# A gated linear-attention kernel: the subtraction of a column maximum moved from two vector engines into an accumulating DMA, and one more batch's attention in float32

## The chip, the cores and the metric

The kernel runs on one core of a Trainium2 chip. The metric is the device time of one execution in microseconds (us). A core has five engines with an instruction queue each: TensorE (PE, matrix products; PEld is its weight load), VectorE (DVE), ScalarE (ACT), GpSimd (POOL) and SyncE (SP), which here only issues DMA transfers. Each engine takes its instructions in the order in which they stand in its queue; an instruction that waits holds up all behind it. 16 DMA engines move data between the chip's memory (HBM) and the on-chip memory.

## The reference

Eight batches, eight heads, 576 tokens, head size 64 (512 channels in all), everything float32:

```python
q_s = exp(q - max(q, axis=-1));  q_s /= sum(q_s, axis=-1) + 1e-9     # softmax over the 64 channels of a head
k_s = exp(k - max(k, axis=2));   k_s /= sum(k_s, axis=2) + 1e-9      # softmax over the 576 tokens
kv  = einsum('bhsd,bhse->bhde', k_s, v)
x   = einsum('bhsd,bhde->bhse', q_s, kv)                             # heads put side by side: 512 channels
gate = sigmoid(causal 5-tap convolution of x over tokens, one filter per channel)
out  = (gate * (x @ w_val)) @ w_out
```

The maximum of k that matters here is taken for each of the 512 channels over 576 tokens; it is one row of 512 numbers for a batch.

## The kernel before, in words

A batch's tokens lie on the 128 partitions as four blocks of 128, and a tail of 64 (two batches share one tail tile). The program is a list of steps, `ORDER`, written out in full in the source: each step is a small function that issues the instructions of one tile, with a letter for the engine where there is a choice (`v` DVE, `a` ACT, `p` POOL). Every engine gets its instructions in the order of that list, and so does the DMA queue of SP.

One batch b goes through these steps. `load_q`, `load_v`, `load_k` (1 MB each, all from SP); `q_max`, `q_sub`, `q_exp`, `q_sum`, `q_mul` make the softmax of q. For k: `load_km b j` loads four tiles with channels on partitions, `k_peak` reduces each to its maxima (DVE), `k_row` writes the 512 maxima as one row to HBM, `k_spread` reads that row back onto all 128 partitions, `k_sub` (POOL or DVE, five per batch) subtracts it from the k tile, `k_exp` (ACT) takes the exponential. `kv` is the product of k and v on PE, `kv_norm` its division by the sums; `q_turn` and `q_turned` transpose q; `attend` (four per batch) makes x in PSUM. From each x tile come `x_high` and `x_low` (a rounded part and the rest, so that float32r products keep the accuracy), `first` and four `tap`s (the convolution; `tap v` is one DVE instruction, `tap a` is a product on ACT and a sum on POOL), and `sigmoid`. `value` (four per batch, 24 matmuls each, line 542) needs all `x_high` and `x_low` of its batch; `gated` multiplies by the gate, `g_high` and `g_low` split again, `project` (four per batch, 24 matmuls each, also line 542) needs all of these, and `store` copies and writes out.

Batches 0 and 1 take k another way (`load_kc`, `k_top`, `k_raise`, `k_turn`), with channels on partitions and a transposition on PE. `F32_BATCHES` names the batches whose `attend` is one float32 product instead of three float32r ones; for the others `kv_high`, `kv_low` and `q_low` prepare the parts. In the first 50 us the weights are also unpacked (`load_words`, `part`, `field`, `scaled`, `signed`, `joined`, `w_high`, `w_low`).

k, q and v tiles have two buffers each, the shared k tail one, the km tiles three (shared with the unpacking of weights).

## Time and profile before

| what | us |
|---|---|
| median of 3 runs (321.49 to 322.12) | 322.0 |
| the profiled execution | 320.3 |
| its span, first to last instruction | 318.5 |
| PE busy | 297.3 (93%) |
| DVE busy | 271.5 (85%) |
| ACT busy | 204.6 (64%) |
| POOL busy | 188.7 (59%) |
| first `value` product starts at | 45.55 |

The lines of the profile give an engine, an operation, the tile written and the tiles read, the shape, and how often. Behind the bar stand the busy time and the mean of one instruction in ns, then the idle time of the engine just before and what ended it.

### The profile page before, as it was taken

The numbers are of one execution on the slowest core, as the hardware profiler recorded it, in microseconds if no ns is written. First come the engines' busy times: TensorE is split into PE (matmuls) and PEld (weight loads), VectorE is DVE, ScalarE is ACT, GpSimd is POOL, SyncE is SP. The second block draws the span as 40 slices with busy tenths as digits, with TensorE's granted clock in tenths as the row PEclk, the third lists the DMA queues.
The fourth block names the chain that finished last, engine by engine and source line by source line (L and its number), as shares of the span: only waits on it lengthen the run. The fifth ranks groups of instructions, "written<-read, shape, count | busy, mean of one in ns | idle before, by whom it ended". The sixth has DMA issues, their size and how long they took to land.

```text
span 318.5 us, 6426 instructions
## 1 busy us (share of the span) xinstructions
PE 297.3 (93%) x2557; PEld 276.4 (87%) x2557; DVE 271.5 (85%) x374; ACT 204.6 (64%) x316; POOL 188.7 (59%) x157
## 2 busy tenths in 40 slices
PE   2897689989899989999999999999999999999995
PEld 1455579979798979889999999999999999999995
DVE  3899999997897999899987979899999979868530
ACT  1789999566967599648973886569543773433201
POOL 2355667979767839867686766674758352311500
PEclk9799999999999999999999999999999999999999
DMA  7995996506897253843427168309201120012012
GB/s 250 370 390 174 410 396 199 194 8 175 238 264 264 74 181 139 254 189 112 143 64 313 50 232 283 160 16 355 82 0 37 39 77 2 0 74 76 0 42 108
DMA packets 20525, 51.25 MB, mean 161 GB/s; under 512 B 2832, under 2 KB 7312, under 8 KB 17808
## 3 DMA queue, kind: packets, MB, share of 16 engines
q1 hardware_dynamic: 20496, 50.85, 46.8%
q8 instruction: 20, 0.33, 0.4%
q14 instruction: 9, 0.07, 0.1%
HBM read 41.39 MB, written 9.45 MB: 160 GB/s over the span
## 4 chain that ended last, share of the span: by engine, by line
PE 55%; DVE 19%; DMA 16%; issue 4%; ACT 4%; SPq 1%; DVEq 0%; ACTq 0%
PE out L542 22%; PE val L542 20%; DVE gate L524 5%; DMA km<-in_k_strided 5%; PE x L498 4%; PE kv L433 4%; DMA words<-in_w_out 3%; DMA out<-o 2%; DMA q<-in_q 2%; DMA q<-in_q_tail 2%; PE qTps L465 2%; DVE qm L347 2%; DVE g L563 2%; DVE qs L362 2%; DVE kpk L274 2%
## 5 line engine op out<-in xcount | busy, mean ns | idle before, releaser
L524 DVE SCALAR_TENSOR_TENSOR gate<-x,cw,gate 128x575 f32<-128x575 f32 (+3 forms) x99 | 78.0, 807 | 3.3 <-POOL gate L528 1.5
L528 POOL TENSOR_TENSOR gate<-gate,far 128x572 f32<-128x572 f32 (+3 forms) x29 | 39.5, 1363 | 39.2 <-ACT far L527 38.9
L542 PE MATMUL out<-gh,w_out_lo 128*128 128x288 f32 x256 | 57.0, 301 | 0.7 <-ACT gh L160 0.7
L542 PE MATMUL val<-xh,w_val_lo 128*128 128x288 f32 x256 | 56.5, 302 | 0.8 <-DVE o L162 0.7
L542 PE MATMUL out<-gl,w_out_hi 128*128 128x288 f32 x256 | 55.6, 296 | 0.9 <-DVE gl L571 0.9
L542 PE MATMUL val<-xl,w_val_hi 128*128 128x288 f32 x256 | 55.0, 296 | 0.9 <-DVE xl L518 0.9
L542 PE MATMUL out<-gh,w_out_hi 128*128 128x288 f32 x256 | 55.4, 295 | 0.0
L542 PE MATMUL val<-xh,w_val_hi 128*128 128x288 f32 x256 | 54.8, 295 | 0.0
L571 POOL TENSOR_TENSOR gl<-g,gh 128x576 fp32r<-128x576 f32 x25 | 36.8, 1476 | 29.5 <-ACT gh L160 23.1
L542 PEld LDWEIGHTS out<-gl,w_out_hi 128*128 128x128 f32 x256 | 41.4, 188 | 1.4 <-DVE gl L571 1.4
L542 PEld LDWEIGHTS val<-xh,w_val_lo 128*128 128x128 f32 x256 | 40.9, 188 | 1.8 <-DVE o L162 0.9
L542 PEld LDWEIGHTS val<-xl,w_val_hi 128*128 128x128 f32 x256 | 41.2, 188 | 1.2 <-DVE xl L518 1.2
L542 PEld LDWEIGHTS out<-gh,w_out_lo 128*128 128x128 f32 x256 | 41.2, 189 | 1.0 <-ACT gh L160 1.0
L542 PEld LDWEIGHTS out<-gh,w_out_hi 128*128 128x128 f32 x256 | 41.5, 188 | 0.0
L542 PEld LDWEIGHTS val<-xh,w_val_hi 128*128 128x128 f32 x256 | 41.3, 188 | 0.0
L389 POOL TENSOR_TENSOR q<-q,qs 128x512 f32<-128x512 f32 x25 | 26.2, 1070 | 14.7 <-DVE qs L364 14.7
L563 DVE TENSOR_TENSOR g<-val,gate 128x576 f32<-128x576 f32 x32 | 23.9, 749 | 9.9 <-PE val L542 7.3
L527 ACT ACTIVATE far<-x,cw 128x572 f32<-128x572 f32 (+3 forms) x29 | 21.0, 737 | 14.2 <-DVE gate L524 9.3
L160 ACT CAST gh<-g 128x576 fp32r<-128x576 f32 x25 | 16.7, 672 | 17.5 <-DVE g L563 17.4
L160 ACT COPY o<-out 128x576 f32<-128x576 f32 (+1 forms) x22 | 13.5, 618 | 22.1 <-PE out L542 12.1
L531 ACT ACTIVATE gate<-gate 128x576 f32<-128x576 f32 x32 | 21.6, 685 | 6.1 <-DVE gate L524 3.5
L289 POOL TENSOR_TENSOR k<-k,kmax 128x512 f32<-128x512 f32 x18 | 24.9, 1397 | 0.9 <-DMA kmax<-krow 0.9
(103 smaller groups left out, 590.1 us busy)
## 6 DMA issues: line engine op xcount, KB each, us to landing
out<-o SPq DMA_DIRECT2D x31, 288.0 KB, 2.3
v<-in_v SPq DMA_DIRECT2D x8, 1040.0 KB, 7.7
q<-in_q SPq DMA_DIRECT2D x7, 1024.0 KB, 7.4
km<-in_k_strided SPq DMA_DIRECT2D x24, 288.0 KB, 3.2
k<-in_k SPq DMA_DIRECT2D x6, 1024.0 KB, 7.5
kc<-in_k_channels SPq DMA_DIRECT2D x8, 288.0 KB, 8.1
words<-in_w_val SPq DMA_DIRECT2D x4, 512.0 KB, 8.9
words<-in_w_out SPq DMA_DIRECT2D x4, 512.0 KB, 11.8
```

Of the source, the lines that this page charges most:

```text
L160: nc.scalar.copy(out=out, in_=in_)
L289: engine(e).tensor_sub(kk[r, cs], kk[r, cs], mx[r, cs])
L389: engine(e).tensor_mul(qq, qq, s.unsqueeze(2).broadcast_to([P, H, D]))
L433: nc.tensor.matmul(acc[h * D:(h + 1) * D, p, :], T["k", b][:, c, cs] if c < 4 else ktz[b % 2][:, cs], T["v", b][:, c, hd] if c < 4 else T[ ...
L498: nc.tensor.matmul(ps[:, :MAIN], a, z, start=(i == 0), stop=(i == len(parts) - 1))
L524: nc.vector.scalar_tensor_tensor(out=a, in0=x, scalar=w, in1=a, op0=ALU.mult, op1=ALU.add)
L527: nc.scalar.activation(part, x, AF.Copy, scale=w)
L528: nc.gpsimd.tensor_add(a, a, part)
L531: nc.scalar.activation(T["gate", b, p], T["gate", b, p], AF.Sigmoid)
L542: nc.tensor.matmul(ps[:, cs], a[:, kb, ms], z[kb][:, cs], start=(kb == 0 and i == 0), stop=(kb == NB - 1 and i == 2),)
L563: nc.vector.tensor_mul(T["g", b, m], T["val", b, m], T["gate", b, m])
L571: engine(e).tensor_sub(T["gl", b, m], T["g", b, m], T["gh", b, m].bitcast(F32))
```

## The change

For batches 2 to 7 the five `k_sub` steps go, and `load_k` and `load_kt` with them. `k_peak` negates its maxima (24 small DVE instructions more). `k_spread` writes the negated row from HBM into all four blocks of the k tile itself (1 MB in place of 256 KB) and into the batch's half of the tail tile (128 KB). A new step `k_add` then issues two DMA transfers from POOL that read k (1 MB) and its tail (128 KB) from HBM and add them onto what lies in the tiles. `k_exp` is as before. In place of the kmax tile there is none.

Batch 1 joins the batches whose `attend` is one float32 product, so its `kv_high`, `kv_low` and two `q_low` go.

The whole list of steps is written anew; 83 taps instead of 99 are on DVE, 45 instead of 29 on ACT and POOL.

```diff
-F32_BATCHES = (0,)
+F32_BATCHES = (0, 1)
...
-    def load_k(b, h="a"):
-        if ("k", b) not in T:
-            T["k", b] = big.tile([P, 4, C], F32, tag="k", name=f"k{b}")
-        nc.sync.dma_start(out=T["k", b][:, :, cols(h)], in_=k[b, :, :, cols(h)])
-
-    def load_kt(b):
-        if b % 2 == 0:
-            T["kt", b] = T["kt", b + 1] = big.tile([P, C], F32, tag="kt", name=f"kt{b}", bufs=1)
-            nc.sync.dma_start(out=T["kt", b], in_=kt[b // 2])
...
-        nc.vector.tensor_reduce(out=T["kpk", b][:, j:j + 1], in_=T["km", b, j], axis=AX.X, op=ALU.max)
+        m = T["kpk", b][:, j:j + 1]
+        nc.vector.tensor_reduce(out=m, in_=T["km", b, j], axis=AX.X, op=ALU.max)
+        nc.vector.tensor_scalar_mul(m, m, -1.0)
...
-        t = T["kmax", b] = small.tile([P, C], F32, tag="kmax", name=f"kmax_{b}", bufs=1)
-        nc.sync.dma_start(out=t, in_=T["krow", b].rearrange("(o n) -> o n", o=1).broadcast_to([P, C]))
-
-    def k_sub(b, i, e="p", h="a"):
-        mx, cs = T["kmax", b], cols(h)
-        kk, r = (T["k", b][:, i], slice(0, P)) if i < 4 else (T["kt", b], rows(b))
-        engine(e).tensor_sub(kk[r, cs], kk[r, cs], mx[r, cs])
+        row = T["krow", b].rearrange("(o n) -> o n", o=1)
+        if ("k", b) not in T:
+            T["k", b] = big.tile([P, 4, C], F32, tag="k", name=f"k{b}")
+        nc.sync.dma_start(out=T["k", b], in_=row.unsqueeze(1).broadcast_to([P, 4, C]))
+        if ("kt", b) not in T:
+            T["kt", b] = T["kt", b + 1] = big.tile([P, C], F32, tag="kt", name=f"kt{b}", bufs=1)
+        nc.sync.dma_start(out=T["kt", b][rows(b)], in_=row.broadcast_to([64, C]))
+
+    def k_add(b):
+
+        nc.gpsimd.dma_start(out=T["k", b], in_=k[b], accum_op=ALU.add)
+        nc.gpsimd.dma_start(out=T["kt", b][rows(b)], in_=kt[b // 2, rows(b)], accum_op=ALU.add)
```

Two places of the new order bear on the prediction. The first is DVE ahead of the first `value` product: the last thing which that product needs is `xl_3` of batch 0. Before, this stood there (kpk is the tile of a batch's maxima, e the unpacked weights, gate the convolution):

```order
L518 TENSOR_TENSOR xl_2_535<-x_2_462,xh_2_522 128x576
L443 TENSOR_SCALAR ks_539<-kv_465 128x4
L444 RECIPROCAL ks_539<-ks_539 128x4
L524 SCALAR_TENSOR_TENSOR gate_2_512<-x_2_462,cw,gate_2_512 128x574
L518 TENSOR_TENSOR xl_3_555<-x_3_515,xh_3_531 128x576
L524 SCALAR_TENSOR_TENSOR gate_3_537<-x_3_515,cw,gate_3_537 128x575
L563 TENSOR_TENSOR g_0_586<-val_0_561,gate_0_417 128x576
```

Now:

```order
L510 TENSOR_TENSOR xl_2_491<-x_2_462,xh_2_485 128x576
L260 TENSOR_REDUCE kpk_238<-km_1_460 128x1
L261 TENSOR_SCALAR kpk_238<-kpk_238 128x1
L234 TENSOR_SCALAR e_420<-e_420 128x512
L235 SCALAR_TENSOR_TENSOR e_420<-words_401,e_420 128x512
L510 TENSOR_TENSOR xl_3_558<-x_3_540,xh_3_543 128x576
L516 SCALAR_TENSOR_TENSOR gate_3_545<-x_3_540,cw,gate_3_545 128x575
L555 TENSOR_TENSOR g_0_586<-val_0_561,gate_0_434 128x576
```

Three of batch 2's four maxima, each with its negation, now stand ahead of `xl_3`; before, all four stood behind it.

The second place is POOL around batch 3's k, between the `g_low` steps of batch 1 (gl) that `project` of batch 1 needs. Before:

```order
L571 TENSOR_TENSOR gl_2_1190<-g_2_1139,gh_2_1181 128x576
L289 TENSOR_TENSOR k_377<-k_377,kmax_1106 128x512
L571 TENSOR_TENSOR gl_3_1248<-g_3_1231,gh_3_1237 128x576
L351 TENSOR_TENSOR q_1187<-q_1187,qm_1233 128x512 x4
L289 TENSOR_TENSOR k_377<-k_377,kmax_1106 128x512
L528 TENSOR_TENSOR gate_0_1239<-gate_0_1239,far_0_1_1341 128x573
```

Now:

```order
L563 TENSOR_TENSOR gl_2_1216<-g_2_1154,gh_2_1174 128x576
L280 DMA k_1140<-in_k 128x2048
L281 DMA kt_846<-in_k_tail 64x512
L563 TENSOR_TENSOR gl_3_1243<-g_3_1220,gh_3_1228 128x576
L520 TENSOR_TENSOR gate_0_1241<-gate_0_1241,far_0_3_1274 128x575
L520 TENSOR_TENSOR gate_0_1241<-gate_0_1241,far_0_2_1302 128x574
```

The subtractions are gone, and two DMA issues stand between `gl_2` and `gl_3`.

More of the change, by code (lines that the diff above doesn't have):

```diff
@@ L133 @@
[L133 to L135 removed]
+    load_q 0 0 2, load_ident, q_max 0 0 2, load_words 1, part 1 a, field 1, q_lift 0 0, q_peak 0 0 2, q_top 0 0 2 a,
+    load_words 8, scaled 1 p, load_kc 0 0, field 8, load_q 0 2 5, load_words 2, load_kc 0 2, k_top 0 0, signed 1,
@@ new lines @@
+    w_low 6 p, k_spread 2, x_low 1 1, q_sub 2 3 p, store 0 1 a, tap 1 1 1 v, sigmoid 1 0, q_sub 2 4 p, tap 1 1 0 v,
+    q_sub 2 0 p, k_peak 3 2, store 0 0 v, attend 1 3, x_high 1 3 a, load_km 3 0, q_sub 2 1 p, sigmoid 1 1,
+    first 1 3 a, attend 1 2, x_high 1 2 a, first 1 2 a, q_max 3, tap 1 3 3 v, k_add 2, x_low 1 2, project 0 2,
+    k_peak 3 0, tap 1 2 3 v, q_exp 2, load_km 5 1, store 0 2 v, load_km 3 3, load_km 4 2, x_low 1 3, q_sum 2,
+    project 0 3, q_sub 3 1 p, value 1 1, tap 1 2 2 a, store 0 3 a, k_peak 3 3, gated 1 1, k_exp 2, k_row 3,
@@ new lines @@
+    q_low 2 0, attend 2 1, first 2 1 a, q_low 2 1, g_low 1 2 p, x_high 2 1 a, gated 1 3, load_km 4 0, k_peak 4 3,
+    tap 2 1 3 v, tap 2 1 2 v, g_high 1 3 a, k_add 3, attend 2 0, x_low 2 1, x_high 2 0 a, first 2 0 a, g_low 1 3 p,
+    tap 2 1 1 v, project 1 2, store 1 2 v, tap 2 0 3 a, project 1 0, tap 2 0 2 a, project 1 3, k_exp 3, tap 2 1 0 v,
+    k_peak 4 1, tap 2 0 1 v, x_low 2 0, store 1 0 v, tap 2 0 0 a, attend 2 3, k_peak 4 0, q_exp 3, load_km 5 2,
+    load_km 7 2, q_sum 3, first 2 3 a, k_row 4, store 1 3 a, load_q 4, x_high 2 3 a, load_km 6 3, tap 2 3 3 a,
@@ new lines @@
+    attend 3 1, k_peak 5 3, gated 2 2, attend 3 0, g_high 2 1 a, first 3 1 a, g_high 2 2 a, q_sub 4 0 p, tap 3 1 3 v,
+    q_sub 4 1 p, q_sub 4 4 p, first 3 0 a, value 2 3, tap 3 1 2 v, load_q 5, tap 3 0 3 v, x_high 3 1 a, x_high 3 0 a,
+    g_low 2 1 v, gated 2 3, tap 3 0 2 v, g_high 2 3 a, q_sub 4 3 p, g_low 2 2 p, g_low 2 3 v, q_exp 4, x_low 3 0,
+    x_low 3 1, project 2 3, warm 0, load_km 6 0, k_row 5, q_max 5, tap 3 1 1 v, project 2 0, store 2 3 a, project 2 1,
+    tap 3 1 0 v, attend 3 2, k_add 4, tap 3 0 1 a, k_exp 4, load_v 4, tap 3 0 0 a, k_peak 7 2, store 2 1 a, q_sum 4,
@@ new lines @@
+    sigmoid 3 3, q_turned 4 1 a, q_turned 4 0 a, tail_turned 4 a, q_sub 5 3 p, q_sub 5 0 v, g_low 3 1 p, q_low 4 1,
+    value 3 2, k_add 5, q_low 4 0, g_low 3 0 p, k_peak 6 3, load_km 7 0, sigmoid 3 2, value 3 3, k_peak 7 3, load_q 6,
+    attend 4 1, gated 3 2, g_high 3 2 v, load_v 5, gated 3 3, first 4 1 a, g_low 3 2 v, g_high 3 3 a, q_max 6,
+    x_high 4 1 a, g_low 3 3 p, tap 4 1 3 v, attend 4 0, tap 4 1 2 v, tap 4 1 1 v, q_sub 6 2 p, first 4 0 a, x_low 4 1,
+    project 3 0, project 3 2, q_sub 6 0 p, x_high 4 0 a, tap 4 0 3 a, store 3 0 a, tap 4 1 0 v, tap 4 0 2 v,
@@ new lines @@
+    warm 0, q_sub 6 1 v, q_turn 5 0, q_turn 5 1, value 4 3, k_peak 7 0, load_q 7, q_turned 5 1 a, value 4 2,
+    q_turned 5 0 v, kv_high 5 a, g_high 4 1 a, q_low 5 0, g_high 4 0 a, g_low 4 1 p, kv_low 5 p, q_low 5 1,
+    sigmoid 4 2, k_row 6, attend 5 0, gated 4 3, g_high 4 3 v, g_low 4 0 p, attend 5 1, load_v 7, gated 4 2,
+    x_high 5 0 a, g_high 4 2 v, x_low 5 0, g_low 4 3 v, q_max 7, x_high 5 1 a, g_low 4 2 p, first 5 1 a, first 5 0 a,
+    k_spread 6, tap 5 0 3 v, tap 5 1 3 a, load_km 7 1, project 4 3, k_add 6, tap 5 1 2 v, project 4 1, tap 5 0 2 v,
@@ new lines @@
+    tap 5 3 0 v, q_mul 6 3 a, value 5 2, q_mul 6 0 p, sigmoid 5 2, tail_turn 6, g_high 5 0 v, kv_high 6 a,
+    tail_turned 6 a, g_low 5 0 v, q_turn 6 0, kv_low 6 p, q_turn 6 1, q_turned 6 0 a, gated 5 2, k_row 7,
+    q_turned 6 1 a, value 5 3, q_low 6 0, g_high 5 2 a, q_low 6 1, attend 6 1, g_low 5 2 v, sigmoid 5 3, g_high 5 1 v,
+    x_high 6 1 a, g_low 5 1 v, attend 6 0, gated 5 3, g_high 5 3 v, x_high 6 0 a, k_spread 7, first 6 0 a, x_low 6 0,
+    k_add 7, g_low 5 3 p, tap 6 0 3 v, project 5 2, first 6 1 a, tap 6 1 3 v, q_exp 7, store 5 2 v, tap 6 1 2 v,
@@ new lines @@
+    q_turned 7 0 a, g_high 6 1 a, q_low 7 0, q_turn 7 1, g_high 6 0 a, value 6 2, sigmoid 6 3, g_low 6 0 p,
+    store 5 1 v, attend 7 1, gated 6 2, g_low 6 1 p, q_turned 7 1 a, x_high 7 1 a, value 6 3, first 7 1 a, q_low 7 1,
+    tap 7 1 3 a, attend 7 0, g_high 6 2 v, gated 6 3, first 7 0 a, g_low 6 2 v, g_high 6 3 a, g_low 6 3 v,
+    tap 7 1 2 a, project 6 3, tap 7 0 3 v, x_low 7 1, tap 7 0 2 v, tap 7 0 1 a, tap 7 1 1 v, tap 7 1 0 a, project 6 2,
+    x_high 7 0 a, tap 7 0 0 a, store 6 3 v, attend 7 2, project 6 1, first 7 2 a, store 6 2 v, tap 7 2 3 v,
```

164 lines of the change are left out of this document (61 added, 103 removed).

## The prediction

> **What bounds the kernel now.** I read first the table of busy time by stretch, cut where the work changes character:
>
> ```profile
> core 0: us, PE busy (x) PEld busy (x) DVE busy (x) ACT busy (x) POOL busy (x), PEclk, DMA share, GB/s
> 0.00:45.50 45.50, 33.54 (x277) 20.69 (x277) 37.97 (x66) 35.45 (x65) 22.25 (x26) 0.96 0.90 327
> 45.50:90.00 44.50, 41.31 (x357) 39.45 (x357) 40.96 (x55) 32.00 (x53) 35.77 (x29) 1.00 0.59 173
> 90.00:145.00 55.00, 52.53 (x442) 49.81 (x437) 51.13 (x67) 41.06 (x72) 41.04 (x34) 1.00 0.58 193
> 145.00:310.00 165.00, 164.57 (x1456) 161.35 (x1456) 140.71 (x189) 95.25 (x127) 89.61 (x70) 1.00 0.30 104
> 310.00:318.50 8.50, 5.30 (x40) 5.06 (x39) 0.76 (x1) 0.80 (x2) 0.00 (x0) 1.00 0.29 104
> ```
>
> Up to 45.5 us the weights are unpacked and batches 0 and 1 are prepared; the DMA engines are 90% busy and DVE works 37.97 of 45.5 us. From the first `value` product on, PE is the limit: it idles 44.50 - 41.31 = 3.2 us, then 2.5 us, and from 145 to 310 us only 0.4 us. So the span is the start of that product, the PE work after it, about 6.1 us of gaps that lie almost all before 145 us, and a tail. What a freed engine is worth after 145 us is next to nothing. What the gaps before 145 us wait for is in the table of waits, restricted to 45.5 to 145 us:
>
> ```profile
> DVE kpk L274 <- DMA km<-in_k_strided: 4.1, 4, 1.8
> DVE qm L347 <- DMA q<-in_q: 1.7, 1, 1.7
> PE x L498 <- DVE qTlo L475: 1.1, 2, 0.7
> PE x L498 <- ACT far L527: 1.1, 1, 1.1
> PE val L542 <- DVE xl L518: 0.9, 1, 0.9
> PE out L542 <- DVE gl L571: 0.9, 1, 0.9
> PE val L542 <- DVE o L162: 0.7, 1, 0.7
> ```
>
> PE's waits end mostly on DVE, and DVE itself, over 90% busy there, loses 5.8 us to loads (4.1 to km tiles, 1.7 to q). The start is read from the timelines of PE and DVE:
>
> ```profile
> 45.55 0.52 PE L542 MATMUL val<-xh,w_val_lo 128*128 128x288 f32 x2
> ...
> 48.56 0.51 PE L542 MATMUL val<-xl,w_val_hi 128*128 128x288 f32 x2
> 47.74 0.75 DVE L518 TENSOR_TENSOR xl<-x,xh 128x576 fp32r<-128x576 f32 x1
> ```
>
> The product's last part begins at 48.56, right after DVE's last `xl` ends at 48.49: the start is paced by DVE's queue.
>
> **The change, part by part.** All durations are from these groups:
>
> ```profile
> L289 POOL TENSOR_TENSOR k<-k,kmax 128x512 f32<-128x512 f32 x18 | 24.9, 1397 | 0.9 <-DMA kmax<-krow 0.9
> L289 POOL TENSOR_TENSOR kt<-kt,kmax 64x512 f32<-64x512 f32 x5 | 6.5, 1297 | 2.9 <-DMA kmax<-krow 2.8
> L289 DVE TENSOR_TENSOR k<-k,kmax 128x512 f32<-128x512 f32 x6 | 6.3, 1047 | 0.0
> L274 DVE TENSOR_REDUCE kpk<-km 128x1 f32<-128x576 f32 x24 | 17.7, 742 | 4.1 <-DMA km<-in_k_strided 4.1
> L308 DVE TENSOR_SCALAR ktop<-ktop 128x1 f32<-128x1 f32 x8 | 1.2, 154 | 0.3
> L524 DVE SCALAR_TENSOR_TENSOR gate<-x,cw,gate 128x575 f32<-128x575 f32 (+3 forms) x99 | 78.0, 807 | 3.3 <-POOL gate L528 1.5
> ```
>
> *Subtractions.* POOL loses 24.9 + 6.5 = 31.4 us and DVE 6.3 us (and one tail). The 24 negations cost DVE 24 x 0.154 = 3.7 us, priced by the same operation on `ktop`. Moving 16 taps takes 16 x 0.807 = 12.9 us from DVE. But that relief is late: ahead of the first product of batch 3 the new list has 43 DVE taps where the old has 45, three `k_sub` fewer and two `q_low` fewer, but 17 negations and more copies; counted out with the rows' means DVE's work there falls by only about 1.4 us. The rest falls where PE has 0.4 us to give, and I count it at nothing; PE's own products cover it.
>
> *The start.* Ahead of the last `xl` of batch 0 the new DVE queue has three maxima with negation (3 x 0.896 = 2.7 us) and about 2 us of other steps that ACT had, and three taps fewer (-2.4 us): counted out with the means, 2.2 us more. Against it, less is loaded before that point. Bounds: 0 (the maxima fill waits for loads) and +2.2; I take **+1.3**, nearer to the upper end because DVE is already busy 37.97 of 45.5 us.
>
> *Batch 1 in float32.* Its four `attend` change from three float32r matmuls to one float32 product, seen as two instructions:
>
> ```profile
> 44.45 1.12 PE L498 MATMUL x<-qT,kvd 128*128 128x512 f32 x2 [0.69 <-DVE gate L524]
> 60.55 0.63 PE L498 MATMUL x<-qT,kvs 128*128 128x512 f32 x2
> 61.02 0.39 PE L498 MATMUL x<-qTlo,kvs 128*128 128x512 f32 x1
> 61.25 0.33 PE L499 MATMUL x<-qTt,kvd 128*128 128x64 f32 x2
> L475 DVE TENSOR_TENSOR qTlo<-qTps,qT 128x1024 fp32r<-128x1024 f32 x14 | 16.7, 1214 | 0.5 <-ACT qT L160 0.5
> ```
>
> 1.12 us against 61.25 - 60.55 = 0.70, so 4 x 0.42 = **+1.7** of PE work after the start. DVE is spared 2 x 1.214 = 2.4 us, which is in the count of 1.4 above.
>
> *The spread and the add.* The nearest rows are the loads of 1 MB, of the row, and of the small spread:
>
> ```profile
> k<-in_k SPq DMA_DIRECT2D x6, 1024.0 KB, 7.5
> kmax<-krow SPq DMA_DIRECT2D x6, 256.0 KB, 4.8
> krow<-kpk SPq DMA_DIRECT2D x6, 2.0 KB, 4.1
> L293 ACT ACTIVATE k<-k 128x2048 f32<-128x2048 f32 x6 | 11.6, 1926 | 0.0
> L294 ACT ACTIVATE ktz<-kt 64x512 f32<-64x512 f32 x6 | 3.8, 626 | 1.3 <-POOL kt L289 1.3
> 289.72 12.80 PE val L542 x96
> ```
>
> A spread of 1 MB I price like a 1 MB load, 7.5 us. An accumulating transfer does not stand in this trace. It moves at least what a load moves (7.5 us to landing); it has to fetch the tile as well as the source, so I bound it above by two loads in a row, 15 us, and take 1.5 loads, 11 us, since three streams move in place of two. Does this fit? Between `k_add` and `kv` the order holds on PE, for batches 2, 3 and 7 (the closest), four products (12.8 us, the last row, from the chain of waits), four products and three `attend` (15.4), three and two (11.3); 1.93 + 0.63 us of that is `k_exp`. That leaves 10.2, 12.9 and 8.8 us for an add of 11, and POOL, 59% busy before and 31 us lighter, reaches its step ahead of PE. So I count it as hidden, by PE's own products. Uncovered it costs what the rival below costs. On POOL the 12 issues replace the 31.4 us; SP's issues take 0.3 to 0.4 us, a POOL instruction 1.3, so between 4 and 16 us, and POOL stays lighter either way. Behind `k_add` on POOL wait the next `g_low`; on SP the spread queues behind a load of q or v.
>
> The Trainium skill, page "DMA: Bandwidth & Descriptors", section "Anatomy of one DMA — SWDGE (gpsimd) path", fits a transfer issued from GpSimd as 2.0 us plus its bytes over 436 GB/s, an estimate of 4.4 us for this one. The measured loads of that size, issued from SP among other traffic, took 7.5, so I do not lean on it; by it the add would be hidden with more to spare and the sum would be the same.
>
> *The gaps.* Batch 2's km tiles are loaded before the weights are done and its maxima taken early, and later km loads stand further ahead of their use, so the 4.1 us DVE loses to them, and part of the 1.7, should go. Since DVE's work hardly falls before 145 us but its waits do, and PE's start comes later while DVE's does not, PE should find DVE further ahead. Of 6.1 us of gaps (some 1.5 us more by restarts, each seen about 0.15 us longer from start to start than as idle) I take **-5.5**; bounds 0 and -7.
>
> *The tail.* The old list ends on half an output tile, the new on a whole one:
>
> ```profile
> L160 ACT COPY o<-out 128x576 f32<-128x576 f32 x20 | 12.7, 639 | 16.8 <-issue 9.0 <-PE out L542 6.8 <-DMA out<-o 0.9
> L160 ACT COPY o<-out 128x288 f32<-128x288 f32 x2 | 0.8, 400 | 5.3 <-PE out L542 5.3
> out<-o SPq DMA_DIRECT2D x31, 288.0 KB, 2.3
> out<-o SPq DMA_DIRECT2D x2, 144.0 KB, 1.7
> ```
>
> 0.24 + 0.6 = **+0.8**.
>
> *The sum.* 1.3 + 1.7 + 0.8 - 5.5 = -1.7 us. The span goes from 318.5 to 316.8, a profiled execution from 320.3 to 318.6. The median of the runs shown is 322.0, 1.7 above the profiled one, so I forecast **320.3**.
>
> **The rivals.**
>
> *The added k comes too late (slower).* Place: ACT's `k_exp`, then PE's `kv`, and behind `k_exp` on ACT the rounding copies and sigmoids of the batch at work. It decides once an add takes more than some 10 us from POOL's turn to landing, or POOL's turn comes late because the 1 MB spread has not landed. At the bound of 15 us batches 2, 3 and 7 would be late by 4.8, 2.1 and 6.2 us, 13 in all; POOL's lead gives back perhaps half, so +6 on the forecast: 326. For it: nothing in the trace bounds an accumulating transfer, and the DMA engines move 6 x 896 KB more. Against: they are under 60% busy after 45.5 us. The Trainium skill, page "SBUF — State Buffer", section "Who interferes with whom", adds that a transfer issued from GpSimd can stall while DVE holds the port pair both use; no row here shows how long.
>
> *The gaps only move (slower).* Start, float32 and tail cost +3.8, and the gaps close by less than 2 us because DVE's work before 145 us is the same: 322 + 2 to 3.8, about 325.
>
> *It cancels.* Gaps close by 3 to 4.5 us: 322.0.
>
> *All of it closes (faster still).* The start is not later and all gaps go: 1.7 + 0.8 - 7 = -4.5, about 317.
>
> That the change does not do what it says is excluded for the parts on the engines: the instructions are in the order. Whether the adding costs no compute engine's time is seen on POOL.
>
> **How the numbers follow.** Forecast 0.38 (its own range 318.5 to 321.3), all closes 0.12, cancels 0.14, gaps only move 0.18, k too late 0.18. About 0.2% (0.6 us) is what a measurement of this kernel tells from no change. Faster is the first two, 0.50; same 0.14; slower 0.36. The range runs from 316 (all closes) to 326.5 (k too late at its half price), which leaves about 0.1 on either side.
>
> **What would show it.** In the changed profile: the first `value` product near 46.8 us (45.55 before) with an `xl` of DVE ending just before its last part; `attend` of batch 1 at 1.1 us; POOL near 175 us with no line of `k_sub`; km waits of DVE under 1.5 us; PE idle from the first product to 145 us near 1 us in place of 5.7. Wrong would be: `k_exp` waiting for a DMA, with PE's `kv` behind it; POOL waiting for the spread for microseconds with a `g_low` behind; an add landing after more than 12 us; or PE gaps of more than 3 us that end on DVE.

## The result, and the profile after

The changed kernel takes 331.99 us (median of 4 runs, 330.39 to 336.0), the kernel before beside it 321.75 (4 runs, 318.31 to 322.12). The ratio is 1.0344, with a 95% interval of 1.0293 to 1.0396: slower by 3.4%. The forecast was 320.3, between 316 and 326.5; the sign is wrong and the time lies outside the range. The profiled execution took 332.45 us, its span 330.3. (Three profiles further below, of e6_early, e14_oldsub and e19_aside, come from executions 1.6 to 2.1% above the fastest of their kernel; they are read for places and releasers, not for sizes.)

The table of busy time by stretch, cut at the first `value` product (51.7 us) and then as in the prediction (start and end of the stretch; its length; busy time and count of PE, PEld, DVE, ACT, POOL; granted clock; DMA share; GB/s):

```profile
core 0: us, PE busy (x) PEld busy (x) DVE busy (x) ACT busy (x) POOL busy (x), PEclk, DMA share, GB/s
0.00:51.70 51.70, 38.16 (x261) 24.70 (x261) 42.45 (x72) 36.11 (x75) 31.16 (x33) 0.77 0.76 265
51.70:90.00 38.30, 36.73 (x260) 34.29 (x259) 36.63 (x51) 28.10 (x47) 29.86 (x25) 1.00 0.60 174
90.00:145.00 55.00, 51.55 (x481) 49.90 (x480) 45.05 (x68) 38.53 (x61) 35.41 (x32) 0.94 0.85 222
145.00:322.00 177.00, 173.78 (x1510) 170.13 (x1509) 135.72 (x186) 113.59 (x179) 89.78 (x74) 0.99 0.50 132
```

Two things stand out against before. The first product starts 6.2 us later (51.75 us, before 45.55). And PE idles 3.4 us between 90 and 145 us and 3.2 us after 145, where DVE and ACT now have room: DVE is busy only 45.05 of 55 us. The DMA engines are 85% and 50% busy in those stretches (58% and 30% before), at 222 and 132 GB/s. The two idle times are two single gaps. The timeline of the changed kernel around them (start, duration, engine, line, what; in brackets the idle time before and what ended it):

```profile
82.70 1.02 POOL L280 DMA_DIRECT2D k<-in_k  x1
...
85.73 1.28 SPq L254 DMA_DIRECT2D km<-in_k_strided  x2
...
91.15 1.91 ACT L285 ACTIVATE k<-k 128x2048 f32<-128x2048 f32 x1 [4.63 <-DMA k<-in_k]
...
93.91 0.75 DVE L260 TENSOR_REDUCE kpk<-km 128x1 f32<-128x576 f32 x1 [4.60 <-DMA km<-in_k_strided]
...
94.77 0.75 DVE L555 TENSOR_TENSOR g<-val,gate 128x576 f32<-128x576 f32 x1
...
95.61 1.14 PE L425 MATMUL kv<-v,k 128*64 128x65 f32 x16 [3.39 <-issue]
...
100.15 0.85 PE L534 MATMUL val<-xh,w_val_lo 128*128 128x288 f32 x2
...
220.91 0.89 POOL L280 DMA_DIRECT2D k<-in_k  x1 [3.66 <-DMA k<-krow]
...
229.18 1.92 ACT L285 ACTIVATE k<-k 128x2048 f32<-128x2048 f32 x1 [3.75 <-DMA k<-in_k]
...
233.52 0.62 ACT L155 COPY o<-out 128x576 f32<-128x576 f32 x1
...
234.19 0.63 PE L534 MATMUL val<-xh,w_val_lo 128*128 128x288 f32 x2 [3.16 <-ACT o L155]
```

*Batch 2.* POOL issues the add at 82.70; it lands 8.4 us later, and ACT waits 4.63 us for it. Beside it SP loads two km tiles of 288 KB at 85.73, and the first takes until 93.9: 8.2 us, where the median before was 3.2. DVE waits 4.60 us for that tile; behind it stands the `gated` step (94.77) that frees a PSUM bank, and only then PE's `kv` of batch 2 starts. Two engines are held, each by a transfer, and the later of the two, DVE, sets PE: `k_exp` is done at 93.73, `gated` at 95.52, and `kv` starts at 95.61. (The profile names no releaser for this `kv`, only "issue"; that it waits for the bank is read from the order of the banks in the kernel and from these times.)

*Batch 6.* POOL reaches its step and waits 3.66 us for the spread; the add lands 8.3 us later, ACT waits 3.75 us for it, and behind `k_exp` on ACT stands the store copy that frees the bank for the next `value` product.

Behind each gap PE runs at a low granted clock for a while: `kv` of batch 2 takes 100.15 - 95.61 = 4.5 us where 2.48 is usual, and the product from 234.19 takes 5.0 where 3.25 is usual, together some 3.7 us more.

The groups and the DMA issues that answer to the prediction's rows (DMA issues: count, size, median us from issue to landing; queue: packets, MB, share of the 16 engines' time):

```profile
L285 ACT ACTIVATE k<-k 128x2048 f32<-128x2048 f32 x6 | 11.5, 1912 | 10.9 <-DMA k<-in_k 10.9
L280 POOL DMA_DIRECT2D k<-in_k x6 | 5.5, 909 | 6.5 <-DMA k<-krow 6.5
L281 POOL DMA_DIRECT2D kt<-in_k_tail x6 | 6.9, 1151 | 0.0
L260 DVE TENSOR_REDUCE kpk<-km 128x1 f32<-128x576 f32 x24 | 17.8, 740 | 4.9 <-DMA km<-in_k_strided 4.8
```

```profile
q0 software_dynamic: 1344, 7.08, 12.0%
...
k<-krow SPq DMA_DIRECT2D x6, 1024.0 KB, 10.3
k<-in_k POOLq DMA_DIRECT2D x6, 1024.0 KB, 8.3
```

An add lands 8.0 to 12.4 us after its issue, a spread of 1 MB after 10.3. The adds move 7.08 MB and take 12.0% of the DMA engines' time.

The span grew by 11.8 us: +6.2 up to the first product; +5.0 from there to PE's last product (269.8 us before, 274.8 now); +0.6 in the tail. The 6.2 us are the difference of two single executions. In the seven profiles with the beginning of the kernel before (that kernel and six runs below; e2_addonly lacks one load there) the first product starts at 45.0 to 48.1 us, in the seven with the changed beginning at 49.4 to 51.9; the medians, 46.4 and 51.0, lie 4.6 apart.

### The profile page after: what moved, and what is told of

Its sections match the earlier page's. It is cut to its first block, busy times and chain, and to the rows that moved or that the text cites. A ratio compares the mean times of both kernels' runs of the same rounds, so it can differ in the third digit from the quotient of the medians.

```text
span 330.3 us, 6423 instructions
## 1 busy us (share of the span) xinstructions
PE 304.7 (92%) x2537; PEld 283.3 (86%) x2537; DVE 260.6 (79%) x376; ACT 217.0 (66%) x361; POOL 186.2 (56%) x161
## 3 DMA queue, kind: packets, MB, share of 16 engines
q0 software_dynamic: 1344, 7.08, 12.0%
## 4 chain that ended last, share of the span: by engine, by line
PE 52%; DVE 18%; DMA 15%; ACT 9%; issue 2%; POOL 2%; SPq 1%; ACTq 0%; DVEq 0%; POOLq 0%
PE val L534 23%; PE out L534 18%; PE x L490 4%; DVE gate L516 4%; DMA k<-krow 4%; DMA km<-in_k_strided 3%; DMA words<-in_w_val 3%; PE kv L425 3%; PE qTps L457 3%; DMA k<-in_k 2%; DVE qs L354 2%; DMA q<-in_q 2%; DVE kpk L260 1%; DVE xl L510 1%; ACT far L519 1%
## 5 line engine op out<-in xcount | busy, mean ns | idle before, releaser
L520 POOL TENSOR_TENSOR gate<-gate,far 128x572 f32<-128x572 f32 (+3 forms) x45 | 60.1, 1338 | 58.4 <-ACT far L519 57.6
L516 DVE SCALAR_TENSOR_TENSOR gate<-x,cw,gate 128x574 f32<-128x574 f32 (+3 forms) x83 | 65.7, 807 | 2.3 <-ACT gate L504 1.0
L534 PE MATMUL val<-xh,w_val_lo 128*128 128x288 f32 x256 | 57.7, 307 | 4.1 <-ACT o L155 3.2
L534 PE MATMUL val<-xh,w_val_hi 128*128 128x288 f32 x256 | 55.8, 300 | 0.0
L534 PEld LDWEIGHTS val<-xh,w_val_hi 128*128 128x128 f32 x256 | 42.3, 193 | 0.0
L563 POOL TENSOR_TENSOR gl<-g,gh 128x576 fp32r<-128x576 f32 x17 | 25.4, 1495 | 28.3 <-ACT gh L155 20.7
L555 DVE TENSOR_TENSOR g<-val,gate 128x576 f32<-128x576 f32 x32 | 24.0, 755 | 21.8 <-PE val L534 18.9
L519 ACT ACTIVATE far<-x,cw 128x572 f32<-128x572 f32 (+3 forms) x45 | 33.0, 742 | 11.7 <-DVE gate L516 11.4
L425 PE MATMUL kv<-v,k 128*64 128x65 f32 x512 | 25.1, 257 | 6.6 <-issue 3.4
L425 PEld LDWEIGHTS kv<-v,k 128*64 128x64 f32 x512 | 22.8, 170 | 7.9 <-issue 3.9
L504 ACT ACTIVATE gate<-x,cw 128x576 f32<-128x576 f32 x25 | 18.5, 747 | 12.3 <-PE x L491 12.3
## 6 DMA issues: line engine op xcount, KB each, us to landing
k<-krow SPq DMA_DIRECT2D x6, 1024.0 KB, 10.3
```

The lines of the kernel that those rows point to most:

```text
L425: nc.tensor.matmul(acc[h * D:(h + 1) * D, p, :], T["k", b][:, c, cs] if c < 4 else ktz[b % 2][:, cs], T["v", b][:, c, hd] if c < 4 else T[ ...
L504: nc.scalar.activation(a, x, AF.Copy, scale=w)
L516: nc.vector.scalar_tensor_tensor(out=a, in0=x, scalar=w, in1=a, op0=ALU.mult, op1=ALU.add)
L519: nc.scalar.activation(part, x, AF.Copy, scale=w)
L520: nc.gpsimd.tensor_add(a, a, part)
L534: nc.tensor.matmul(ps[:, cs], a[:, kb, ms], z[kb][:, cs], start=(kb == 0 and i == 0), stop=(kb == NB - 1 and i == 2),)
```

## The experiments

Three explanations were open. Theory 1: the late start comes from a low clock that TensorE is granted between 10 and 50 us. Theory 2: it comes from VectorE's queue. Theory 3: the chain of row, spread and add comes late at batches 2 and 6. Ratios are against the kernel before, run in turn with each on the same chip.

### The start and the places: e1_busy, e9_later, e10_both, e6_early

e1_busy keeps TensorE busy where it idled:

```diff
-warm 0, k_top 1 0, ..., kv 0
+warm 16, k_top 1 0, ..., kv 0
-k_turn 1 1
+busy ktps 1 8, k_turn 1 1
-attend 0 2
+busy xps 0 12, attend 0 2
```

> The changed kernel with TensorE kept busy where it idled early: 16 transposes of the identity (written to a bank nobody reads) ahead of kv of batch 0, 8 more ahead of the second k_turn of batch 1, 12 more ahead of the third attend of batch 0. Theory 1, the late start comes from TensorE's low granted clock between 15 and 50 us: the clock goes back to 1.0 from 28 us on, kv of batches 0 and 1 take 2.5 us instead of 4.4 and 4.2, the first value product starts near 47.5 us and the kernel takes about 327.5. Theory 2, the late start comes from VectorE's queue, which is full from 21 us on and ends the last xl of batch 0 at 54.7 us: the clock rises too, but that xl ends where it ended (54.5 to 55) and the kernel takes 331 to 332.5.

Measured: 339.7 us, ratio 1.059 (1.050 to 1.068), worse by more than 2% and outside both expectations. The clock did rise (1.00 from 30 to 40 us), but the 12 transposes, written into an unused part of an x tile's bank, waited 5.0 us for DVE to finish with that tile, and the first product came at 54.55. The edit brought a wait of its own, so this run says little on the clock.

e9_later moves five steps behind the last `xl`:

```diff
-..., field 6, ..., k_peak 2 1, ..., scaled 6 p, ..., part 5 a, ..., signed 5, x_low 0 3
+..., x_low 0 3, k_peak 2 1, field 6, scaled 6 p, part 5 a, signed 5
```

> The changed kernel with five steps moved from ahead of the last xl of batch 0 to right behind it: one maximum of batch 2 with its negation, and the unpacking of one slab and a half of w_out (field 6, scaled 6, part 5, signed 5), some 3.0 us of VectorE by the profile of the changed kernel. Theory 2 (VectorE's queue sets the start): the last xl ends about 2 to 3 us earlier, at 52 to 52.7, held then by the attend in front of it (51.7 in the slow clock, and a copy of 0.64 behind it), and the kernel takes 329 to 330. Theory 1 (the clock sets the start): the xl moves by no more than 0.5 us and the time stays at 331.5 to 332.5.

Measured: 336.8 us, 1.050 (1.041 to 1.059). The last `xl` ended 1.0 us earlier, but the steps moved behind it stand ahead of the first `gated`, and PE waited 4.5 us for that. VectorE has no free place up to 60 us: what is taken from one product's path lands on the next one's.

e10_both has both edits.

> Both edits of the two runs before it. If the start is set by VectorE's queue and next to it by TensorE's clock: the last xl of batch 0 ends 3 us earlier, near 51.5, and the kernel takes 328 to 329.5, less than with either edit alone. If one of them alone sets it: the time of that one alone. If batches 2 and 6 absorb what the start gains (their maxima and adds are as late as before): no gain over 331.

Measured: 343.7 us, 1.074 (1.065 to 1.083): the losses of both add up.

e6_early moves the chain at batches 2 and 6:

```diff
-k_peak 7 0, load_q 7, ..., k_row 6, ..., load_v 7, ..., k_spread 6
+k_peak 7 0, k_row 6, k_spread 6, load_q 7, ..., load_v 7
-q_sub 2 3 p, q_sub 2 4 p, q_sub 2 0 p, ..., q_sub 2 1 p, ..., k_add 2
+k_add 2, q_sub 2 3 p, q_sub 2 4 p, q_sub 2 0 p, ..., q_sub 2 1 p
```

> The changed kernel with three things moved earlier: on SP the writing of the row of batch 6 and its spread ahead of the loads of q and v of batch 7; on POOL the add of batch 2 ahead of that batch's q_sub steps. Nothing else is moved. Theory 3 (the chain row, spread, add comes late at batches 2 and 6 by its place in SP's and POOL's queues, and the two gaps of 3.4 and 3.2 us on TensorE, each with some 1.8 us of low clock behind it, come from it): ScalarE's wait for the add falls from 4.6 and 3.7 us to under 1, both gaps shrink below 1 us, and the kernel takes 322 to 325. Rival (the adds and spreads are slow because of what they share the DMA engines with, wherever they stand): the adds of batches 2 and 6 land within 1.5 us of where they landed, or other loads are late in their place, and the kernel takes 329 to 332.

Measured: 333.6 us, 1.031 (1.019 to 1.043), no better than the changed kernel. At batch 6 the gap is gone. At batch 2 the add was issued at 79.1 us, ahead of two km loads issued at 80.2, and took 10.0 us to land; what came late in place of the add was km. Timeline of e6_early:

```profile
89.84 0.75 DVE L259 TENSOR_REDUCE kpk<-km 128x1 f32<-128x576 f32 x1 [6.53 <-DMA km<-in_k_strided]
...
92.23 0.85 PE L533 MATMUL val<-xh,w_val_lo 128*128 128x288 f32 x2 [5.98 <-DVE o L156]
```

The two km loads landed 9.6 and 10.0 us after their issue. So the rival holds at batch 2: an earlier add moves the wait from ACT to DVE.

This run also speaks against theory 1. Its program is the changed kernel's up to some 60 us, but this execution was granted a higher clock there. Stretches of the changed kernel, then of e6_early (the clock is the number behind the five busy times):

```profile
10.00:20.00 10.00, 9.44 (x23) 4.18 (x23) 8.94 (x19) 4.64 (x7) 4.41 (x4) 0.66 1.06 387
20.00:30.00 10.00, 6.80 (x63) 4.94 (x63) 9.68 (x16) 9.92 (x28) 8.86 (x8) 0.64 1.04 399
```

```profile
10.00:20.00 10.00, 9.44 (x20) 3.61 (x20) 8.98 (x17) 3.57 (x6) 2.75 (x2) 1.00 1.06 387
20.00:30.00 10.00, 7.51 (x89) 5.37 (x89) 8.17 (x14) 9.83 (x27) 9.32 (x8) 0.89 1.04 398
```

With 1.00 and 0.89 in place of 0.66 and 0.64, the first product stood at 51.75 us in both; in e14_oldsub, with the same beginning and 1.00 up to 20 us, at 51.91. VectorE lost time of its own in this execution (8.17 us busy from 20 to 30 us, 9.68 in the changed kernel), so the pair alone does not say that the clock is worth nothing. But over the profiles with this beginning the start does not follow the clock: the earliest, 49.37 us in e16_freed, had 0.83 and 0.74 in these two stretches. The clock is not what makes the start late.

### The parts of the change: e2_addonly, e3_f32, e4_plain, e5_nospread

e2_addonly puts only the adding into the order of before (`k_peak`, `k_spread` and `k_add` as in the change), for batch 2 so and for the others alike:

```diff
-load_k 2, ..., load_kt 2, ..., k_sub 2 2 p, ..., k_sub 2 0 p
+k_add 2
```

> The kernel before, in its own order, with only the adding put in: load_k, load_kt and the k_sub steps go, the maxima are negated, the row is spread over the k tile, and the add is issued from POOL where the first k_sub of that batch stood. Batch 1's attention stays as it was. Theory 3 (the chain of row, spread and add is what costs, whatever the order): the add lands 15 to 20 us after the spread is issued (10 and 8 in the changed kernel), where the old spread and five subtractions took 4.8 and about 7; k_exp comes 4 to 7 us later at each of the six batches, PE waits for kv at two to four of them, and the time is 326 to 336. Rival (the new order of the steps is what costs, and the adding alone is free or a gain, since DVE loses 6.3 us and POOL 31 us of work): 318 to 322.

Measured: 350.4 us, 1.090 (1.082 to 1.099), far above even the slower expectation. Its largest waits for transfers (us in total, times, longest):

```profile
POOL k L279 <- DMA k<-krow: 37.3, 5, 10.8
...
DVE kpk L259 <- DMA km<-in_k_strided: 18.9, 4, 6.6
```

POOL stands for up to 10.8 us in front of its add because the spread has not landed, with its `q_sub`, `g_low` and tap sums behind; DVE waits 18.9 us for km tiles, 4.1 before.

e3_f32 is the other half of the change alone:

```diff
-F32_BATCHES = (0,)
+F32_BATCHES = (0, 1)
...
-kv_high 1 a, ..., kv_low 1 p, ..., q_low 1 0, ..., q_low 1 1
```

> The kernel before, in its own order, with batch 1's attention alone in float32 (its kv_high, kv_low and two q_low gone). Four products of 1.12 us in place of 0.70 cost PE 1.7 us, four steps of DVE, ACT and POOL go (3.6 us of DVE among them) between 45 and 90 us, where DVE is full. If PE's own work sets the time: 322.0 + 1.7 = 323.7. If DVE's work there is worth as much as PE's: 321 to 322.5.

Measured: 321.5 us, 1.001 (0.997 to 1.005). It costs nothing that can be measured: 1.7 us of PE against the DVE time that it spares.

e4_plain takes the accumulation out and leaves everything else:

```diff
-        nc.gpsimd.dma_start(out=T["k", b], in_=k[b], accum_op=ALU.add)
+        nc.gpsimd.dma_start(out=T["k", b], in_=k[b])
```

(and the same for the tail).

> The changed kernel with the two transfers of each add as plain copies (no accumulation) from the same queue, at the same places, behind the same spread. It leaves out the subtraction of the maximum of k for batches 2 to 7. If it is the accumulation that is slow and holds up the loads beside it: the copy of 1 MB lands in 5 to 7 us in place of 8.3, the km tile of 8.2 us at batch 2 in 4 to 5, the gap ahead of kv 2 falls from 3.4 to under 1.5 us, the one at batch 6 from 3.2 to under 1, and the kernel takes 325 to 328. If it is the amount of transfers and the place of the steps: the copies land within 1 us of the adds and the kernel takes 330 to 333.

Measured: 322.2 us (10 runs, 321.2 to 323.5), 1.004 (1.000 to 1.008). This one word is worth 9.8 us, more than expected: 332.0 with it, 322.2 without, at the same places and with the same bytes. DMA view of e4_plain, then its timeline at batch 2:

```profile
q0 software_dynamic: 1152, 7.08, 6.4%
...
k<-in_k POOLq DMA_DIRECT2D x6, 1024.0 KB, 5.7
```

```profile
86.95 1.92 ACT L285 ACTIVATE k<-k 128x2048 f32<-128x2048 f32 x1 [2.00 <-DMA k<-in_k]
...
88.69 0.76 DVE L260 TENSOR_REDUCE kpk<-km 128x1 f32<-128x576 f32 x1 [1.06 <-DMA km<-in_k_strided]
...
90.60 0.69 PE L425 MATMUL kv<-v,k 128*64 128x65 f32 x16
```

Half the engine time for the same 7.08 MB (6.4% for 12.0%), a landing of 5.7 us for 8.3, ACT's wait 2.00 for 4.63, DVE's for km 1.06 for 4.60, and no gap in front of `kv`. PE has no single gap over 0.9 us between 50 and 300 us. In the two profiles (spans 330.3 and 319.1 us) 2.0 us of the difference lie ahead of the first product, where nothing is added yet; of the other 9.2, PE's waits give 5.2 (8.2 against 3.0) and the slow clock behind the two big gaps some 3.7.

The two km loads beside the add of batch 2, 8.2 us in the changed kernel, take 4.6 to 4.9 here. That holds for this place and not for all loads. The rows of all 24 km loads, first of the changed kernel, then of e4_plain:

```profile
km<-in_k_strided SPq DMA_DIRECT2D x24, 288.0 KB, 4.2
```

```profile
km<-in_k_strided SPq DMA_DIRECT2D x24, 288.0 KB, 4.5
```

The median is no longer beside accumulations than beside copies, and single km loads take up to 10.4 and 10.6 us in the two. A general slowing of the loads by the accumulation is not shown.

e5_nospread drops the spread as well:

```diff
-        nc.sync.dma_start(out=T["k", b], in_=row.unsqueeze(1).broadcast_to([P, 4, C]))
-        nc.sync.dma_start(out=T["kt", b][rows(b)], in_=row.broadcast_to([64, C]))
```

> As the run before it, and without the spread of the row (1 MB and 128 KB of transfers less for each batch; the row itself is still written). It leaves out the subtraction of the maximum of k for batches 2 to 7. The copy then waits only for its k tile and POOL's turn. If the spread's 10 us and its traffic matter: POOL's waits for it (1.7, 3.7 and 1.1 us at batches 3, 6 and 7) are gone, km and q loads land 1 to 3 us sooner, and the time lies 3 us or more under the run before it. If they are hidden: the same time within 1.5 us. What is left over the kernel before (322) in this run is the new order's own and batch 1's float32: I expect 324 to 328, 6 us of it from the later first value product.

Measured: 320.7 us, 1.005 (1.001 to 1.010), the same as e4_plain. Where only plain copies follow it, the spread is hidden, for all its 10 us and 1 MB, though the median km load falls to 3.3 us without it. The time lies below the 324 to 328 that were expected for the new order itself: its later start (49.6 us here) does not come out as 6 us at the end.

### The prize, the order and the start: e12_nosub, e13_hybrid, e14_oldsub, e16_freed

e12_nosub takes the subtractions out of the kernel before:

```diff
-k_sub 2 2 p, k_sub 2 3 p, k_sub 2 4 p, k_sub 2 1 p, k_sub 2 0 p
...
-k_sub 7 1 p, k_sub 7 2 v, k_sub 7 3 p, k_sub 7 0 p, k_sub 7 4 p
```

> The kernel before, in its own order, with all k_sub steps dropped (the loads, the row and its spread of 256 KB stay). It leaves out the subtraction of the maximum of k for batches 2 to 7. It measures the prize: what 31.4 us of POOL and 6.3 us of DVE are worth when nothing is paid for them. As the prediction counted (covered by PE's products): 321 to 322.5. If the gaps of TensorE before 145 us come from these steps: 316 to 319.

Measured: 318.7 us (10 runs), 0.988 (0.983 to 0.993). The prize is 1.2%, some 3.8 us, and not the nothing that the prediction gave it.

e13_hybrid exchanges the beginning of the changed kernel's order:

```diff
-load_q 0 0 2, load_ident, q_max 0 0 2, load_words 1, part 1 a, field 1, q_lift 0 0, q_peak 0 0 2
...
+load_kc 0 1, load_q 0 0 2, load_words 8, k_top 0 1, load_ident, q_lift 0 0, q_max 0 0 2, q_peak 0 0 2
...
-value 0 0, gated 0 0, kv_norm 1 a, k_peak 2 3
+value 0 0, gated 0 0, k_peak 2 2, k_peak 2 0, k_peak 2 1, k_peak 2 3
```

> The changed kernel with the order of the kernel before up to the first value product (without what belongs to k of batches 2 and 3), and its own order from there; the maxima of batch 2 come right behind the first product. Theory 2 (the order ahead of the first product, which keeps VectorE waiting for loads in the first 10 us and gives it 2.7 us of maxima to do, costs the start): the first product starts at 45.5 to 47 and the time falls by 3 to 6 us, to 326 to 329. Rival (what is won at the start is lost again at batch 2, whose maxima, row, spread and add are no earlier): the first product is at 45.5 to 47, the gap ahead of kv 2 grows by as much, and the time stays at 330 to 333.

Measured: 335.3 to 345.9 us in four runs, median 341.7; the profile is of the fastest, 335.3. The start came to 45.26, so the order ahead of it is what sets it. But then PE waited in front of batch 1's attention:

```profile
PE x L489 <- ACT qT L154: 9.9, 1, 9.9
```

ACT stood 12.7 us before a sigmoid for DVE, and DVE waited for km tiles. Neither half fits the other. The rival is right that the gain is lost again, but it is lost at batch 1 and not at batch 2, and the loss is larger than it said.

e14_oldsub puts the five subtractions back, on POOL where the add stood:

```diff
-k_spread 2, ..., k_add 2
+load_k 2, load_kt 2, k_spread 2, ..., k_sub 2 0 p, k_sub 2 1 p, k_sub 2 2 p, k_sub 2 3 p, k_sub 2 4 p
```

> The changed kernel's order with the subtraction as it was before: load_k and the row's spread of 256 KB from SP where the spread of 1 MB stood, five k_sub on POOL where the add stood, no negation. If the accumulating transfer is what costs: about the time of the plain copies, 322 to 325. If the new order lives on POOL's relief (the five steps are 7 us on POOL, with g_low and taps behind them): 327 to 333, with TensorE's waits on POOL's gl and far.

Measured: 334.1 us, 1.029 (1.018 to 1.041). The new order lives on POOL's relief; PE waits 7.1 us in five pieces for POOL's `gl`. In this order the accumulating transfer (1.034) costs as much as the work that it replaces (1.029), within the intervals.

e16_freed is e6_early and, on VectorE:

```diff
-k_peak 3 0, tap 1 2 3 v, ..., load_km 4 2, ..., k_peak 3 3, gated 1 1, k_exp 2, k_row 3
+tap 1 2 3 v, ..., gated 1 1, k_peak 3 0, load_km 4 2, k_peak 3 3, k_row 3, k_exp 2
```

> The run e6_early with one thing more: the two maxima of batch 3 whose tiles are loaded beside batch 2's add, and with them a load and the row of batch 3, stand behind gated 1 1 on VectorE, so that VectorE does not wait for those loads (6.5 us there) with gated behind it. If the add costs by the loads that it slows down beside it: the gap of 6.0 us at 80 to 90 us goes, none over 1.5 us comes in its place, and the time is 324 to 328. If it costs by its own lateness: ScalarE waits for the add as in e6_early (1.7 us) and the gap falls only to 3 to 5 us, time 329 to 333.

Measured: 328.9 us, 1.018 (1.010 to 1.027), better than the changed kernel (the intervals do not overlap). The gap ahead of `kv` 2 is gone once DVE does not stand before those loads, while the early add alone (e6_early) only moved it. So at that place the cost went through the loads beside the add, into an engine that had other work behind the wait. But the time lies between the two expectations, and the first one's "none over 1.5 us comes in its place" does not hold: at 111 us PE waits 3.7 us for POOL's `gl`, which stands behind the add of batch 3, and POOL stood 6.8 us before that batch's spread. ACT waits 10.0 us for adds, 8.2 of it at one. What is left, 1.018 against 1.004 of the plain copies, comes at batches other than 2.

### Length of the chain or hold on the engines: e17_swap, e18_swap_after

Both load k plainly and early, and add the row onto it, so that one transfer stands behind the row and not two. The add in both (and the same for the tail) is:

```diff
+        nc.gpsimd.dma_start(out=T["k", b], in_=row.unsqueeze(1).broadcast_to([P, 4, C]), accum_op=ALU.add)
```

> The kernel before, in its own order, with source and tile of the accumulation exchanged: k is loaded plainly and early as before, and the negated row (2 KB in HBM, read 576 times) is added onto the k tile by one accumulating transfer from POOL where the row's spread of 256 KB stood on SP; the k_sub steps go. As many accumulated bytes as in e2_addonly, but one transfer behind the row in place of two in series. If the length of the chain (10 us of spread and then 8 of add) is what costs: k_exp comes about when it came before (10 to 12 us behind the row's spread; before 4.8 and some 7), and the time is 317 to 323, against 350 of e2_addonly. If the accumulation costs by holding the DMA engines and the loads beside it: 328 to 340.

> The same exchange in the changed kernel's order (with the edits of e16_freed): k is loaded plainly from SP ahead of the row, the accumulating transfer of the row stands on POOL where the spread stood on SP, and the later add goes. If the chain's length costs: ScalarE no longer waits for k at any batch (10.0 us in three waits in e16_freed) and the time is that of the plain copies or less, 319 to 323. If the accumulation's hold on the DMA engines costs: 326 to 330, as e16_freed.

Measured: 342.5 us, 1.067 (1.058 to 1.075), and 331.9 us, 1.035 (1.028 to 1.042). Neither beats before, and both lie above even the slower of their two expectations, though ACT hardly waits for k any more: not at all in e17_swap, 3.1 us once in e18_swap_after. The accumulation now lands 12.9 and 12.8 us after its issue (9.5 to 17.5) and takes 12.6 and 13.3% of the engines. What is late is the rest. From the chain of waits of e18_swap_after (start, length, what):

```profile
84.45 8.49 DMA km<-in_k_strided
...
101.02 8.47 DMA km<-in_k_strided
...
121.76 10.67 DMA q<-in_q_tail
```

Three loads of 256 and 288 KB, 8.5 to 10.7 us each, stand on the chain that ends last. The two km loads run beside an accumulation (issued at 78.40 and 98.70, landed 13.1 and 12.6 us later). The load of the q tail does not, as the next accumulation is issued at 137.69; so a slow load on that chain is not by itself a sign of the accumulation. With the wait for k almost gone, neither run comes near the time of the plain copies: the lateness of k is not all that costs, and the expectation that it would be is refuted. In the order of before one transfer in place of two is worth 8 us (342.5 against 350.4). The exchange is not a clean one, since the accumulation from the row is itself slower, 12.9 us to landing against 8.3.

### The hold alone: e19_aside, e20_aside_plain

Three transfers of 384 KB for each batch, onto a tile that nobody reads; the control has the same line without `accum_op`:

```diff
+        nc.gpsimd.dma_start(out=aside, in_=k[b].rearrange("p c n -> p (c n)")[:, :3 * C // 2], accum_op=ALU.add)
```

> The kernel before without the subtraction (as e12_nosub, and without the row's spread, so it leaves out the subtraction of the maximum of k for batches 2 to 7), plus accumulating transfers whose result nobody reads: three of 384 KB for each batch, issued from POOL where the first, third and fifth k_sub stood, onto a tile put aside. Only the accumulation's traffic and its issues are there; no lateness can come from waiting for it, save POOL's own where the tile put aside is still being written. If the accumulation's hold on the DMA engines is what costs: DVE waits for km, q and stores by several us more than in the next run, and the time is 325 or more, 5 us over the next run. If it is the lateness of the chain: within 1.5 us of the next run, 318 to 321.

> The same with plain copies onto the tile put aside. Control for the run before it: 317 to 321 by either theory; over e12_nosub (318.7) it has 18 issues of some 0.6 us on POOL and 6.9 MB of transfers more.

Measured: 330.1 us, 1.023 (1.013 to 1.034), and 325.0 us, 1.011 (1.005 to 1.018). The single runs do not overlap (326.4 to 331.6 against 324.4 to 325.8), though the intervals do. Queue and the largest POOL wait, first of e19_aside, then of e20_aside_plain:

```profile
q0 software_dynamic: 2592, 7.08, 12.8%
```

```profile
POOL aside L277 <- DMA aside<-in_k: 27.5, 6, 6.0
```

```profile
q0 software_dynamic: 1440, 7.08, 7.0%
```

```profile
POOL aside L277 <- DMA aside<-in_k: 19.0, 5, 5.0
```

By the ratios accumulating costs 1.2%, some 4 us, more than copying, although nobody waits for its data. But POOL, which has to wait until the tile put aside is free, waits 8.5 us longer there, and its 18 issues take 16.0 us for 10.3. The control itself came out above its expectation, presumably for the same reason (not tried). So this run does not separate the hold on the DMA engines from POOL's own time; how the 4 us divide stays open.

No version was found that beats the kernel before and still subtracts the maximum.

## Why the prediction was wrong, step by step

**The step that failed is the sentence "So I count it as hidden, by PE's own products."** The price was not far off: 11 us for the add (bounds 7.5 to 15), measured 8.0 to 12.4. Three things behind the price were missed. It asked only whether k arrives before PE's `kv`, while the engine that waits is ACT, whose store copy sets PE at batch 6. It relied on "POOL ... reaches its step ahead of PE", but POOL was at its step too late at batch 2 (82.70, behind four `q_sub`), when the first of the four products that were to cover the add had run from 79.19 to 82.4, and it stood before an unlanded spread at batches 3, 6 and 7 (6.5 us). Nor was POOL "31 us lighter": the 16 taps moved off DVE brought it 16 sums, 60.1 us in place of 39.5, which the prediction left out. And it took the other transfers as unaffected, while the km load beside the add of batch 2 took 8.2 us. No one of these is the cost alone: in e4_plain POOL stands even longer before spreads, 8.9 us, and that run is at 1.004. e4_plain shows the sum: 9.8 us for the accumulation, at the same places and behind the same waits. How it divides between k that lands late and loads that are held stays open.

**The spread**, priced at 7.5 us, took 10.3. As traffic it is hidden (e5_nospread); as what POOL waits for it is not (37.3 us in e2_addonly).

**The start**, +1.3 in the prediction, came out at +6.2. Over all the profiles it is 4.6 by the medians, still beyond the bound of +2.2, which left out two terms. The product starts on the first parts of x and comes to its last part once VectorE has made the last `xl`, here in the changed kernel:

```profile
51.75 0.51 PE L534 MATMUL val<-xh,w_val_lo 128*128 128x288 f32 x2
...
53.95 0.76 DVE L510 TENSOR_TENSOR xl<-x,xh 128x576 fp32r<-128x576 f32 x1
...
54.76 0.52 PE L534 MATMUL val<-xl,w_val_hi 128*128 128x288 f32 x2
```

The groups of VectorE up to the last `xl`, before (to 48.49 us) and after (to 54.70), show them:

```profile
L240 DVE TENSOR_SCALAR e<-words 128x512 f32<-128x512 f32 x6 | 2.5, 412 | 1.0 <-DMA words<-in_w_val 0.6 <-DMA words<-in_w_out 0.4
```

```profile
L339 DVE TENSOR_REDUCE qm<-q 128x16 f32<-128x1024 f32 (+2 forms) x3 | 5.3, 1751 | 5.1 <-DMA q<-in_q 5.1
L225 DVE TENSOR_SCALAR e<-words 128x512 f32<-128x512 f32 x7 | 4.9, 704 | 2.6 <-DMA words<-in_w_val 2.6
...
L260 DVE TENSOR_REDUCE kpk<-km 128x1 f32<-128x576 f32 x3 | 2.2, 726 | 0.0
L361 DVE TENSOR_SCALAR qm<-qm 128x32 f32<-128x32 f32 x1 | 1.2, 1246 | 0.0
```

The three maxima cost what was counted (2.2 us and 0.5 for the negations). But the same `e<-words` step took 704 ns on average in place of 412, and the negation of batch 1's q maxima 1246 in place of 182: 7 x 0.29 + 1.06 = 3.1 us that no count of steps with old means could show. The 2.0 of the first term stand in every profile with this beginning (704 to 819 ns); the 1.06 only in this one (168 to 177 ns in the others), and the kernel before has 1.0 of the same kind, a step on the taps that took 1133 ns against 178 after. And DVE's idle time up to there rose from 7.6 to 9.7 us, since the new queue begins with q and not with the small tiles of k; the prediction expected less waiting there. DVE's busy time rose from 40.9 to 45.0 us. 4.1 + 2.1 = 6.2. That the order ahead of it sets the start, and the clock does not, is shown by e13_hybrid, and by the starts and clocks under e6_early; that it acts through VectorE is read from its queue, busy 9.4 to 9.9 of every 10 us from 20 to 60 us. How the 3.1 us arise was not tried.

**Batch 1 in float32**: right as a price, counted 1.12 us each, and as an edit it is free (e3_f32). The first of the four in the timeline after:

```profile
63.53 1.02 PE L490 MATMUL x<-qT,kvd 128*128 128x512 f32 x2
```

**The gaps**, -5.5: half right. Those that it named did close; beside the two new ones PE waits only 0.9 us (for DVE's `g`) and 0.7 us (for POOL's `gl`). The two new ones, 3.4 and 3.2 us, cost more than that, and the slow clock behind each was not in the sum at all. Waits of DVE for km were to fall below 1.5 us and are 4.8, of which 4.6 at batch 2 beside the add; in e4_plain they are 3.4, so this sign failed without the accumulation too.

**The subtractions**, "I count it at nothing": wrong by 3.8 us in the kernel's favour (e12_nosub), and the reason with it, as steps off POOL and DVE do close gaps before 145 us: PE idles 3.9 us from the first product to there in the profile of e12_nosub, 5.7 before. Nor did POOL fall to the 175 us that were named as a sign: it is busy 186.2, as the 12 issues (5.5 + 6.9 us) and the 16 sums more take most of the relief.

**The tail**, +0.8: measured +0.6.

In ratios the 3.4% are: -1.2 for the subtractions saved (e12_nosub), 0.1 for float32 (e3_f32), 3.0 for the accumulation (e4_plain against the changed kernel), and the remaining 1.5 for the new order with its late start; the last is a difference and not a measurement of its own, and each of the others is known to about half a point. The "0.6 us" that the prediction took for what tells a change from none was too fine as well: single runs of the kernel before lie between 317.2 and 325.8 us.

Among the rivals, "the added k comes too late" named the place (ACT's `k_exp` and what is behind it) and the sign, and gave 326 at a chance of 0.18. It was too cheap: it counted each batch's own lateness against PE, and nothing for the loads beside or for the slow clock behind a gap. The stall of a POOL transfer under DVE, which it cited from the Trainium skill, is isolated by no run here.

The fit that the prediction took from the Trainium skill, page "DMA: Bandwidth & Descriptors", section "Anatomy of one DMA — SWDGE (gpsimd) path", gave 4.4 us for a transfer of this size from GpSimd. The plain copies came to 5.7 in this traffic, the accumulating ones to 8.3: for an accumulation the measurement decides, and the fit does not cover it.
